# More PSUM banks for the preparing steps of a hash-attention and gated-FFN kernel, a second queue for the first loads, and products of zeros ahead of them

**Chip, cores, metric.** One core of a Trainium2 chip; each group of experiments ran on one chip, side by side with the kernel before. Time is the device time of one execution in microseconds (us), median of several runs.

## The reference

```python
# attention: batch 4, 8 heads, 768 positions, head size 64, 6 hash bits
q_bits = (q @ proj > 0);  k_bits = (k @ proj > 0)          # one bucket number of 6 bits each
mask   = q_bucket[:, None] == k_bucket[None, :]
attn   = softmax(where(mask, q @ k.T / 8, -1e9));  x = attn @ v
# gated block on x reshaped to (3072, 512); d_ff = 1536, weights given as float64
out = ((silu(x @ w_gate) * (x @ w_val)) @ w_out)
```

## The kernel before

There are 16 pairs of heads, four to a batch. Each pair needs eight *preparing steps*: four transposes (q and k, two halves each; PE writes a PSUM bank, ScalarE copies it out) and four hash products (PE writes a bank; ScalarE makes q's signs, VectorE makes k's bits). The steps of pair n+1 are issued during pair n, two in an iteration. An iteration has two scores, two value products ("attend"), and after each half of a pair a row sum ("norm") whose reciprocal VectorE takes out of PSUM. When a batch is done, its gated-block work becomes a list of small pieces ("atoms") issued between the attention work of the next batch. VectorE meanwhile narrows the float64 weights.

```python
sc_ps  = tc.tile_pool(name="sc_ps",  bufs=2, space=PSUM)   # scores, 2 banks each
av_ps  = tc.tile_pool(name="av_ps",  bufs=1, space=PSUM)
aux_ps = tc.tile_pool(name="aux_ps", bufs=1, space=PSUM)   # one bank
mm_ps  = tc.tile_pool(name="mm_ps",  bufs=2, space=PSUM)   # two banks, gated block
def bank(name):      return mm_ps.tile([P, 512], FP32, tag="mm", name=name)
def side_bank(name): return aux_ps.tile([P, 512], FP32, tag="aux", name=name)
...
def front(n, bank=side_bank):                              # the preparing steps
    def transpose(name, half):
        ...
        ps = bank("tps")
        for i in range(CH):
            nc.tensor.transpose(ps[:, i * P : (i + 1) * P], raws[name, n][...], ident)
        nc.scalar.copy(T[name, n][:, half * HQ : (half + 1) * HQ], ps[:, 0:HQ])
    def hash_bits(name, half):
        ps = bank("hps")
        nc.tensor.matmul(ps[:, 0:HQ], hash_w[name], T[name, n][:, cols], ...)
        ...                                                # q: ScalarE, k: VectorE reads ps
...
def norm(u):
    ps = side_bank("sum")                                  # the same bank as the steps
    for h in range(2):
        nc.tensor.matmul(ps[h * D : (h + 1) * D, 0:HQ], ones, t[:, h, :], ...)
    nc.vector.reciprocal(r, ps[:, 0:HQ])
...
for step in front(0, bank):                                # first pair: the two gated banks
    step()
```

The softmax here doesn't subtract the row's maximum and nothing guards it: scores larger than these inputs give would overflow.

## Time and profile before

| | before |
|---|---|
| median of 3 runs | 1187.71 us (1186.89 to 1187.98) |
| span of the profiled run | 1185.9 us |
| TensorE busy / idle | 1156.9 / 29.0 us |
| first score / first gated product start at | 13.25 / 143.37 us |

The lines that carry the argument stand in the prediction below. The way to read them: the busy share says that TensorE is the bound, the slices say *where* it is idle, and the wait rows of that stretch say *on what*. One view more is needed here: the first batch of the kernel before in the view of busy time by stretch. Columns are stretch, its length, then busy time of PE, PEld, DVE, ACT and POOL with instruction counts, granted clock, DMA share and GB/s.

```profile
13.25:143.37 130.12, 110.53 (x626) 46.06 (x625) 94.00 (x125) 58.31 (x84) 3.84 (x7) 0.99 0.29 78
143.37:1185.90 1042.53, 1038.88 (x3838) 522.93 (x3836) 411.92 (x607) 217.62 (x350) 14.55 (x27) 1.00 0.11 31
```

From the first score to the first gated product takes 130.12 us; everything after it 1042.53.

### The profile page before, as it was taken

Reading aid. Unit: us, or ns where it says so; the run is one execution under the profiler, and the core shown is the slowest. Engines: PE = TensorE matmul, PEld = TensorE weight load, DVE = VectorE, ACT = ScalarE, POOL = GpSimd, SP = SyncE. Lnnn points to the kernel's source line nnn. Section 1 sums busy time; section 2 is a strip of 40 time slices with the busy share of each in tenths; the row PEclk is TensorE's granted clock in tenths of the full one; section 3 lists DMA queues with packets and bytes.
Section 4 is the critical chain, followed back from the end, with each engine's and each line's share of the span. In section 5 each row is a group of like instructions: output and inputs, shape, how many; then the busy total and the mean of one; then the engine's idle time right before and its main releaser. Section 6 shows DMA issues by size and latency. Waiting matters only on the chain.

```text
span 1185.9 us, 10899 instructions
## 1 busy us (share of the span) xinstructions
PE 1156.9 (98%) x4480; PEld 573.2 (48%) x4480; DVE 508.2 (43%) x756; ACT 280.3 (24%) x441; POOL 19.2 (2%) x44
## 2 busy tenths in 40 slices
PE   7888899999999999999999999999999999999998
PEld 3333355555544445555554445555554444555543
DVE  3777689998852323343331233333233222222100
ACT  4444422222212222222221213222131211000000
POOL 0000000000000000000000000000000000000000
PEclk9999999999999999999999999999999999999999
DMA  5322222324210120100002012010000000000000
GB/s 142 76 76 76 58 79 92 101 71 113 88 40 18 37 57 1 40 1 1 14 1 58 18 36 49 1 40 1 14 1 1 18 18 18 1 1 0 1 27 27
DMA packets 63698, 44.76 MB, mean 38 GB/s; under 512 B 51872, under 2 KB 55968, under 8 KB 63648
## 3 DMA queue, kind: packets, MB, share of 16 engines
q1 hardware_dynamic: 58752, 26.23, 8.6%
q0 software_dynamic: 4896, 17.83, 4.9%
q8 instruction: 35, 0.57, 0.2%
q14 instruction: 15, 0.12, 0.0%
HBM read 37.76 MB, written 6.29 MB: 37 GB/s over the span
## 4 chain that ended last, share of the span: by engine, by line
PE 97%; DVE 2%; ACT 1%; DMA 0%; SPq 0%; issue 0%; ACTq 0%
PE val L299 21%; PE g L299 21%; PE po L320 21%; PE sc L244 14%; PE av L255 11%; PE hps L213 4%; PE sum L276 2%; PE tps L205 2%; DVE r L279 2%; ACT qb L216 0%; ACT qT L208 0%; DMA kraw<-in_k_dram 0%; SPq L85 0%; ACT A L246 0%; ACT o L324 0%
## 5 line engine op out<-in xcount | busy, mean ns | idle before, releaser
L299 PE MATMUL val<-xT,wv 128*128 128x384 f32 x768 | 266.2, 489 | 0.0
L299 PE MATMUL g<-xT,wg 128*128 128x384 f32 x768 | 265.9, 489 | 0.0
L320 PE MATMUL po<-wo,ht 128*128 128x512 f32 x576 | 257.1, 597 | 0.0
L246 ACT ACTIVATE A<-sc 128x768 f32<-128x768 f32 x192 | 155.5, 812 | 208.2 <-PE sc L244 177.0
L299 PEld LDWEIGHTS val<-xT,wv 128*128 128x128 f32 x768 | 142.5, 190 | 105.4 <-DVE acc L263 6.0
L299 PEld LDWEIGHTS g<-xT,wg 128*128 128x128 f32 x768 | 142.5, 190 | 105.1 <-DVE acc L263 6.0
L320 PEld LDWEIGHTS po<-wo,ht 128*128 128x128 f32 x576 | 106.8, 190 | 134.1 <-issue 130.7
L244 PE MATMUL sc<-qT,kT 64*128 64x384 f32 x768 | 156.0, 485 | 0.0
L279 DVE RECIPROCAL r<-sum 128x384 f32<-128x384 f32 x32 | 81.8, 2556 | 151.9 <-PE sum L276 151.9
L255 PE MATMUL av<-A,vraw 128*64 128x386 f32 x768 | 144.8, 498 | 0.0
L306 DVE SCALAR_TENSOR_TENSOR t<-t,g 128x384 f32<-128x384 f32 x96 | 53.1, 554 | 206.3 <-ACT t L305 206.3
L263 DVE TENSOR_TENSOR acc<-acc,A 128x768 f32<-128x768 f32 x128 | 122.3, 955 | 35.2 <-ACT A L246 30.3
L305 ACT ACTIVATE t<-g 128x384 f32<-128x384 f32 x96 | 47.1, 490 | 351.6 <-PE g L299 347.0
L311 DVE SCALAR_TENSOR_TENSOR ht<-t,val 128x384 f32<-128x384 f32 x96 | 53.1, 553 | 125.0 <-PE val L299 125.0
L255 PEld LDWEIGHTS av<-A,vraw 128*64 128x64 f32 x768 | 49.6, 137 | 82.4 <-issue 81.3
L244 PEld LDWEIGHTS sc<-qT,kT 64*128 64x128 f32 x768 | 69.0, 190 | 21.5 <-issue 21.5
L244 PE MATMUL sc<-qb,kb 64*128 64x384 bf16 x384 | 63.8, 329 | 0.1
L218 DVE TENSOR_SCALAR kb<-hps,above_k,times_k 128x384 bf16<-128x384 f32 x32 | 21.6, 675 | 83.9 <-PE hps L213 83.4
L244 PEld LDWEIGHTS <-kb 64*128 64x128 bf16 x384 | 18.7, 93 | 67.9 <-issue 55.1
L324 ACT COPY o<-po 128x512 f32<-128x512 f32 x24 | 14.0, 585 | 144.3 <-PE po L320 142.0
L216 ACT ACTIVATE qb<-hps,nudge 128x384 bf16<-128x384 f32 x32 | 18.6, 581 | 69.4 <-PE hps L213 69.3
L213 PE MATMUL hps<-qT,hashq 128*128 128x384 f32 x64 | 27.7, 515 | 5.5 <-DVE e L281 5.5
(58 smaller groups left out, 409.9 us busy)
## 6 DMA issues: line engine op xcount, KB each, us to landing
qraw<-in_q_dram SPq DMA_DIRECT2D x32, 192.0 KB, 3.7
kraw<-in_k_dram SPq DMA_DIRECT2D x32, 192.0 KB, 4.6
vraw<-in_v_dram SPq DMA_DIRECT2D x16, 384.0 KB, 3.4
words<-in_moe_w_val_dram POOLq DMA_DIRECT2D x12, 512.0 KB, 3.8
words<-in_moe_w_out_dram POOLq DMA_DIRECT2D x12, 512.0 KB, 3.6
out_dram<-o SPq DMA_DIRECT2D x24, 256.0 KB, 2.0
words<-in_moe_w_gate_dram POOLq DMA_DIRECT2D x10, 512.0 KB, 3.9
words<-in_moe_w_gate_dram SPq DMA_DIRECT2D x2, 512.0 KB, 5.8
```

The lines of the kernel that those rows point to most:

```text
L205: nc.tensor.transpose(ps[:, i * P : (i + 1) * P], raws[name, n][:, half * CH + i, :, :].rearrange("p h d -> p (h d)"), ident)
L213: nc.tensor.matmul(ps[:, 0:HQ], hash_w[name], T[name, n][:, cols], start=True, stop=True)
L244: nc.tensor.matmul(sc[:, h, 0:HQ], x["k", n][rows, ks], x["q", n][rows, qs], start=start, stop=not start)
L246: nc.scalar.activation(ring[u % RING][:, :, 0:HQ], sc[:, :, 0:HQ], AF.Exp, scale=SCALE)
L255: nc.tensor.matmul(ps[h * D : (h + 1) * D, 0:AW], raws["v", n][:, h, c, :], a[:, h, :], start=c == 0, stop=c == NCH - 1)
L263: nc.vector.tensor_tensor(acc[n, half], acc[n, half], a[:, :, 0:HQ], op=ALU.add)
L279: nc.vector.reciprocal(r, ps[:, 0:HQ])
L299: nc.tensor.matmul(ps[:, 0:HQ], w[:, j, f * P : (f + 1) * P], x[:, j, half * HQ : (half + 1) * HQ], start=j == 0, stop=j == NJ - 1)
L305: nc.scalar.activation(t, ps[:, 0:HQ], AF.Tanh, scale=0.5)
L306: nc.vector.scalar_tensor_tensor(out=t, in0=t, scalar=1.0, in1=ps[:, 0:HQ], op0=ALU.add, op1=ALU.mult)
L311: nc.vector.scalar_tensor_tensor(out=ht, in0=now["t"], scalar=0.5, in1=ps[:, 0:HQ], op0=ALU.mult, op1=ALU.mult)
L320: nc.tensor.matmul(ps, hs[half][f][:, i * P : (i + 1) * P], wo[:, f, :], start=f == 0, stop=f == NF - 1)
```

## The change

The intent: in the first batch the gated block has no work yet, so its two PSUM banks lie idle; the preparing steps should rotate over them and the old bank. At start-up, k and the projection should not stand behind q on one queue, and products with zeros before the data comes should bring TensorE's products to their full pace, since the first products of the kernel run slow (three transposes take 0.87 us at 4.79 us and 0.55 later).

```diff
-    def load(n):
+    def load(n, k_queue=nc.sync):
 ...
-    load(0)
+    load(0, nc.scalar)
+    ident = ...; make_identity(nc, ident)           # moved up
+    zeros = konst.tile([P, 512], BF16, tag="zeros", name="zeros")
+    nc.vector.memset(zeros, 0.0)
+    for _ in range(9):
+        ps = bank("idle")
+        nc.tensor.matmul(ps, zeros[:, 0:P], zeros, start=True, stop=True)
+    two_proj = konst.tile([P, NBITS], FP32, tag="proj", name="proj")
+    for o in (0, D):
+        nc.scalar.dma_start(two_proj[o : o + D, :], proj[:, :])
 ...
-        nc.vector.memset(hash_w[name], 0.0)         # and six small loads of proj on nc.sync
+        nc.gpsimd.memset(hash_w[name], 0.0)         # and six small VectorE copies of two_proj
 ...
+    turn = iter(range(1 << 20))
+    def front_bank(name):
+        return side_bank(name) if atoms or next(turn) % 3 == 2 else bank(name)
-    def front(n, bank=side_bank):
+    def front(n):
 ...
-            ps = bank("tps")                        # and bank("hps")
+            ps = front_bank("tps")
 ...
-    for step in front(0, bank):
+    for step in front(0):
```

More of the change, by code (lines that the diff above doesn't have):

```diff
@@ L78 @@
     raws = {}
-    def load(n):
+    def load(n, k_queue=nc.sync):
         b, pr = pairs[n]
-        for name, src in (("q", q), ("k", k)):
+        for name, src, queue in (("q", q, nc.sync), ("k", k, k_queue)):
             t = raw.tile([P, NCH, 2, D], FP32, tag=name + "raw", name=name + "raw")
             for h in range(2):
-                nc.sync.dma_start(t[:, :, h, :],
+                queue.dma_start(t[:, :, h, :],
                                   src[b, 2 * pr + h].rearrange("(p c) d -> p c d", c=NCH))
@@ L93, in load @@
         raws["v", n] = t
-    load(0)
+    load(0, nc.scalar)
+    ident = konst.tile([P, P], FP32, tag="ident", name="ident")
+    make_identity(nc, ident)
+    zeros = konst.tile([P, 512], BF16, tag="zeros", name="zeros")
[6 more added lines that the diff above has]
+        nc.scalar.dma_start(two_proj[o : o + D, :], proj[:, :])
     hash_w = {}
@@ L102 @@
         hash_w[name] = konst.tile([P, P], FP32, tag="hash" + name, name="hash" + name)
-        nc.vector.memset(hash_w[name], 0.0)
-        for o in (0, D):
-            for at in (0, NBITS) if name == "q" else (0,):
-                nc.sync.dma_start(hash_w[name][o : o + D, o + at : o + at + NBITS], proj[:, :])
+        nc.gpsimd.memset(hash_w[name], 0.0)
     def column(name, first, second, third, rest):
@@ L120 @@
     times_k = column("times_k", OFF, -OFF / 2, -NBITS * OFF / 2, 0.0)
-    ident = konst.tile([P, P], FP32, tag="ident", name="ident")
-    make_identity(nc, ident)
     ones = konst.tile([P, D], FP32, tag="ones", name="ones")
     nc.vector.memset(ones, 1.0)
+    for name in "qk":
+        for o in (0, D):
+            for at in (0, NBITS) if name == "q" else (0,):
+                nc.vector.tensor_copy(hash_w[name][o : o + D, o + at : o + at + NBITS],
+                                      two_proj[o : o + D, :])
     RING = 4
@@ L194 @@
     bits = {}
-    def front(n, bank=side_bank):
+    atoms = []
+    turn = iter(range(1 << 20))
+    def front_bank(name):
+        return side_bank(name) if atoms or next(turn) % 3 == 2 else bank(name)
+    def front(n):
         def transpose(name, half):
@@ L211, in hash_bits @@
             cols = slice(half * HQ, (half + 1) * HQ)
-            ps = bank("hps")
+            ps = front_bank("hps")
             nc.tensor.matmul(ps[:, 0:HQ], hash_w[name], T[name, n][:, cols], start=True, stop=True)
@@ L286, in norm @@
             push_ffn(b)
-    atoms = []
     def push_ffn(b):
```

## The prediction

Marked cuts in the recorded texts are statements of hardware behaviour that no trace or run of this case shows, and what hung on them. The prediction's sum came to 15.85 us: 14.1 for the banks, -0.9 for VectorE, 1.75 for start-up, 0.9 for the slow stretch. "The clock" at start-up means the pace of the products: the granted clock reads 1.00 in every us from 4 to 14 of the kernel before. The slow stretch of the kernel before does show in it: 0.60, 0.50, 0.50 and 0.69 in the four us from 114 to 118, 1.00 from 113 to 114 and from 118 to 120.

> **What bounds the kernel now.** I read the page first: the busy shares, the forty slices and the chain that ended last.
>
> ```profile
> PE 1156.9 (98%) x4480; PEld 573.2 (48%) x4480; DVE 508.2 (43%) x756; ACT 280.3 (24%) x441; POOL 19.2 (2%) x44
> ...
> PE   7888899999999999999999999999999999999998
> DVE  3777689998852323343331233333233222222100
> ...
> PE 97%; DVE 2%; ACT 1%; DMA 0%; SPq 0%; issue 0%; ACTq 0%
> ```
>
> TensorE is the bound. Its idle time is 1185.9 - 1156.9 = 29.0 us, and no change that leaves the products alone can gain more than that (and what slow-clock products cost). The row of slices (29.6 us each) puts nearly all the idle time in the first five slices: start-up and the first batch, where no gated-block work fills TensorE's waits. Then the waits of TensorE from 13 to 150 us (what it waited for, total, times, longest):
>
> ```profile
> PE hps L213 <- DVE e L281: 5.5, 4, 1.4
> PE hps L213 <- ACT qb L216: 5.4, 8, 0.7
> PE tps L205 <- ACT qT L208: 4.6, 8, 0.6
> PE tps L205 <- DVE e L281: 4.1, 3, 1.4
> ```
>
> Together 19.6 us. The same view from 150 us to the end is empty. All four rows are of the preparing steps (transposes "tps", hash products "hps"), which share one PSUM bank with each other and with the row sums "sum" that the reciprocal reads. The timeline of TensorE shows single cases (start, duration, and in brackets the idle time before it):
>
> ```profile
> 80.74 0.55 PE L205 MATMUL tps<-ident,qraw 128*128 128x128 f32 x3 [1.36 <-DVE e L281]
> 81.85 0.55 PE L205 MATMUL tps<-ident,kraw 128*128 128x128 f32 x3 [0.57 <-ACT qT L208]
> ...
> 91.84 0.91 PE L213 MATMUL hps<-kT,hashk 128*128 128x384 f32 x2 [0.67 <-ACT qb L216]
> ```
>
> The second step of an iteration waits for ScalarE to empty the bank that the first filled: 0.57 us for a transpose, 0.67 for a hash product. After a row sum the first step waits 1.36 for the 2.56 us reciprocal to leave it. Start-up, in the timeline again:
>
> ```profile
> 4.79 0.87 PE L205 MATMUL tps<-ident,qraw 128*128 128x128 f32 x3 [4.79 <-DMA qraw<-in_q_dram]
> 6.62 0.87 PE L205 MATMUL tps<-ident,kraw 128*128 128x128 f32 x3 [0.95 <-DMA kraw<-in_k_dram]
> ...
> 8.76 1.59 PE L213 MATMUL hps<-qT,hashq 128*128 128x384 f32 x2
> 10.15 1.48 PE L213 MATMUL hps<-kT,hashk 128*128 128x384 f32 x2
> ...
> 13.25 0.34 PE L244 MATMUL sc<-qb,kb 64*128 64x384 bf16 x2
> ```
>
> q lands at 4.8 us, k at 6.6, and the first score starts at 13.25. The reader should see that three transposes take 0.87 us here and 0.55 later, two hash products 1.59 and 0.91 later: the first products run slow. (The granted-clock row shows full speed there, so it does not see this.)
>
> [...]the durations above are long until about 11 us and normal at 12.4. [...]from 113.7 to 117 us scores and value products ran at about half speed (0.99 and 1.49 us for four where 0.81 is usual), just after 3.0 us in which TensorE did only transposes and waited. It cost about 2.70 + 2.11 - 1.72 - 1.52 = 1.6 us. [...]the engines are 0.9 busy from about 2.5 us on, at 220 to 260 GB/s, while SyncE's issues of q and k take 1.35 us each.[...]
>
> **The change, part by part.** The instruction orders compared show the same sequence on every engine; added are nine loads and products of zeros on TensorE, one clearing and six small copies on VectorE, four issues ahead of ScalarE's table load and two clearings on GpSimd. No work is removed.
>
> *Banks.* Until the first gated work is pushed, steps take turns: two steps in the gated block's banks, every third in the old one. So two steps of one iteration never share a bank, and all sixteen waits for evictions go: 8 x 0.57 + 8 x 0.67 = 10.0 us (the two ACT rows). The seven waits for the reciprocal go only where the step does not draw the old bank. I counted the turns: pair 0's preparation takes 0 to 7, the next 8 to 15, and so on; a turn that leaves 2 on division by 3 is the old bank. Steps beside a row sum are the first and last two steps of each preparation (except the first two of pair 1's, which have no sum before them). In order: turn 14 (old bank, first of its two: full wait 1.37); turn 17 (old, second: 1.37 less the 0.48 that the first transpose takes, 0.89); turn 23 (second, behind a hash product of 0.85: 0.52); for pair 3's none; for pair 4's turns 32 and 38, both first: 1.37 each. Left: 3 x 1.37 + 0.89 + 0.52 = 5.5. Removed: 9.6 - 5.5 = 4.1. With the evictions 14.1 us.
>
> *Does VectorE take over?* One pair's period, in the view of busy time by stretch (length, then PE, PEld, DVE, ACT):
>
> ```profile
> 61.50:92.70 31.20, 25.99 (x151) 10.82 (x152) 23.56 (x31) 13.77 (x20) 1.06 (x2) 1.00 0.27 72
> ```
>
> Without waits TensorE needs 26.0 us and VectorE has 23.6 of work: 91%. I followed VectorE through one wait-free pair, using the spacings in its timeline: from a reciprocal at 2.6 us after the iteration's start it finishes the twelfth accumulation about 13.4 us after it, and TensorE wants it for the next row sum at 13.6. That holds, but with no room; narrowing operations of 0.69 instead of 0.43 us push it by some 0.3. I charge 0.3 for each of three pairs: -0.9. ScalarE (13.8 of 26) is no limit: an exponential held up by its ring buffer has a whole iteration before it is read.
>
> *Start-up.* q and k of pair 0 are 0.79 MB; at about 235 GB/s from 2.0 us on, both are in by about 5.7: q 0.9 later than now, k 0.8 earlier. The zeros start near 1.2; a bf16 product of 384 columns takes 0.16 to 0.17 in the trace, so 512 take 0.22, slow 0.44, nine about 4.0: they end near 5.2, before the data. If the clock is up, four transposes take 4 x 0.48 and four hash products 4 x 0.85 (the spacings later in the trace), without eviction waits since three banks rotate: 5.7 + 1.9 + 3.4 = 11.0. Projection and its six copies should be there at 6 to 7, before the hash products at 7.6. I add 0.5 for a chance that the clock is not up yet[...]: first score at 11.5 instead of 13.25, a gain of 1.75.
>
> *The slow stretch.* [...]0.9 of the 1.6, an estimate.
>
> Sum: 14.1 - 0.9 + 1.75 + 0.9 = 15.85. All of it carries to the end, since from 143 us on TensorE waits for nothing: 1187.7 - 15.9 = 1171.8; I say **1171.5 us**, 1.4% less.
>
> **The rivals.** (1) VectorE becomes the bound in the first batch: its late accumulations hold the row sums and, through the ring of four, the exponentials. For it: 91%[...]. Against it: each step's own wait for a hash product lets it catch up, as the 4.3 us gap before "kb" shows now. It would leave perhaps 9 us of the banks' gain: 1177. (2) Start-up gains nothing or loses: q comes later, and zeros that end too early[...] leave the hash products slow: first score at 13 or later, so 1173.5. (3) The pay-back: weights narrowed by VectorE are late for the first "val" product at 146 us, which now waits for its last piece within 0.6 us. A VectorE behind by 1 us would cost at most that: 1172.5. (4) Everything goes well, all reciprocal waits but two shrink and the slow stretch goes: 19 to 20 us, 1167.5.
>
> **Range and chances.** The banks' 14 us are counted waits, uncertain by 2; start-up by 1.2; the clock by 1. Rivals 1 and 2 together make about 1176, rival 4 makes 1167.5: range 1167.5 to 1175.5. Two per cent is 23.8 us, below 1164: it would take nearly all 29 us of idle time. Chances: faster 0.01, same 0.98, slower 0.01.
>
> **What would show it.** In the new trace: TensorE's waits from the first score to the first "g" near 6 us instead of 19.6, with the rows for "qT" and "qb" gone and rows for the reciprocal at five places; a pair's period near 27 to 28 us instead of 31.2; the first score near 11.5 and the first "g" product near 127.5 to 128 instead of 143.4; from there to the end 1042.6 us as before. Wrong: row sums that wait for "acc" by more than 0.5 us each, a first score later than 13, or a tail longer by over 1 us.

## The result

| | before | after |
|---|---|---|
| median | 1187.3 us (4 runs, 1186.25 to 1187.98) | 1168.91 us (4 runs, 1167.45 to 1169.88) |
| profiled span | 1185.9 | 1168.1 |
| first score at | 13.25 | 14.50 |
| first score to first gated product | 130.12 | 110.83 |
| first gated product to the end | 1042.53 | 1042.77 |

The ratio is 0.9845, 95% interval 0.9828 to 0.9862. Ratios here are the mean time of one kernel's fast runs over that of the other's in the same rounds, so they are not quite the ratio of the medians quoted. The gain stays under the 2% from which a change counts as faster. The page of the kernel after, its busy shares and TensorE's slices:

```profile
PE 1155.5 (99%) x4489; PEld 575.1 (49%) x4489; DVE 508.9 (44%) x761; ACT 279.4 (24%) x441; POOL 19.5 (2%) x46
...
PE   8999999999999999999999999999999999999998
```

The eights after the first slice are gone. All of TensorE's waits of the kernel after, over the whole span:

```profile
PE hps L232 <- DVE e L300: 3.2, 3, 1.4
PE tps L224 <- DVE e L300: 2.2, 2, 1.4
PE tps L224 <- DMA kraw<-in_k_dram: 1.3, 1, 1.3
PE idle L105 <- DVE nudge L119: 1.2, 1, 1.2
PE tps L224 <- DMA qraw<-in_q_dram: 0.6, 1, 0.6
```

The rows for evictions (qT, qb) have gone, and five reciprocal waits of together 5.4 us are left, where 19.6 us of waits stood. (The rows name "e", the 0.10 us instruction of VectorE right behind the reciprocal; of the two only the reciprocal reads the bank.) The stretches again:

```profile
14.50:125.33 110.83, 105.22 (x625) 46.25 (x625) 93.94 (x125) 57.40 (x85) 3.84 (x7) 1.00 0.31 79
125.33:1168.10 1042.77, 1038.89 (x3838) 522.98 (x3836) 411.88 (x607) 217.71 (x350) 14.55 (x27) 1.00 0.11 31
```

The first batch is 130.12 - 110.83 = 19.3 us shorter, more than the 14.2 us of wait rows that went: TensorE's idle time falls from 19.6 to 5.6 us, and its busy time too, from 110.53 to 105.22. The tail is the same to 0.24 us. And start-up (timeline of TensorE, start and duration) is 1.25 us *longer*:

```profile
1.19 4.02 PE L105 MATMUL idle<-zeros 128*128 128x512 bf16 x9 [1.19 <-DVE nudge L119]
5.83 0.87 PE L224 MATMUL tps<-ident,qraw 128*128 128x128 f32 x3 [0.62 <-DMA qraw<-in_q_dram]
8.03 0.87 PE L224 MATMUL tps<-ident,kraw 128*128 128x128 f32 x3 [1.32 <-DMA kraw<-in_k_dram]
...
11.25 1.49 PE L232 MATMUL hps<-kT,hashk 128*128 128x384 f32 x2
...
14.50 0.34 PE L263 MATMUL sc<-qb,kb 64*128 64x384 bf16 x2
```

Both data come later than before (q at 5.83 instead of 4.79, k at 8.03 instead of 6.62), and the transposes still take 0.87 us for three: behind the zeros they are no faster.

So two things were to be explained: why the banks gave 19.3 us where the rows promised 14, and why start-up lost.

### The profile page after: what moved, and what is told of

Same layout as the page of the kernel before. It is cut to its first block, busy times and chain, and to the rows that moved or that the text cites. A ratio compares the mean times of both kernels' runs of the same rounds, so it can differ in the third digit from the quotient of the medians.

```text
span 1168.1 us, 10917 instructions
## 1 busy us (share of the span) xinstructions
PE 1155.5 (99%) x4489; PEld 575.1 (49%) x4489; DVE 508.9 (44%) x761; ACT 279.4 (24%) x441; POOL 19.5 (2%) x46
## 4 chain that ended last, share of the span: by engine, by line
PE 97%; DVE 2%; DMA 1%; ACT 0%; issue 0%; ACTq 0%; DVEq 0%
PE val L316 22%; PE g L316 22%; PE po L337 22%; PE sc L263 14%; PE av L274 11%; PE hps L232 4%; PE sum L295 2%; PE tps L224 2%; DVE r L298 1%; DMA kraw<-in_k_dram 1%; DVE acc L282 0%; DVE acc L278 0%; ACT A L265 0%; DVE wv L177 0%; ACTq L85 0%
## 5 line engine op out<-in xcount | busy, mean ns | idle before, releaser
L341 ACT COPY o<-po 128x512 f32<-128x512 f32 x24 | 14.1, 585 | 144.3 <-PE po L337 142.0
L278 DVE SCALAR_TENSOR_TENSOR acc<-A 128x768 f32<-128x768 f32 x32 | 30.5, 952 | 0.8 <-ACT A L265 0.8
```

The source lines that it names most:

```text
L278: nc.vector.scalar_tensor_tensor(out=acc[n, half], in0=ring[(u - 1) % RING][:, :, 0:HQ], scalar=S * EPS / P, in1=a[:, :, 0:HQ], op0=ALU.ad ...
```

## The experiments

**1 and 2: each half of the change alone.** Run e1 takes the kernel before and adds only the rotation; run e2 takes the kernel after and gives back the old bank:

```diff
 e1, against the kernel before
+        return side_bank(name) if atoms or next(turn) % 3 == 2 else bank(name)   # as in the change
 e2, against the kernel after
-        return side_bank(name) if atoms or next(turn) % 3 == 2 else bank(name)
+        return bank(name) if next(turn) < 8 else side_bank(name)
```

Of theory A in e1's text, that a removed wait is worth more than its idle row, the mechanism named for the rest is cut; no trace shows one. The spacings stay.

> Only the bank rotation, start-up as before. Theory A: [...] (in the changed kernel two transposes of one iteration take 0.81 us to the next score instead of 1.59, 0.78 less where the idle row said 0.57; two hash products 1.49 instead of 2.43, 0.94 where the row said 0.67). Then the rotation alone gives 14.2 us of rows, about 3.5 us[...] and perhaps the 1.6 us of the slow stretch: 17.7 to 19.3 less than before, about 1168 to 1169.6 us, and so as fast as the whole change or faster. Rival, the prediction's sum: 14.1 less 0.9 for VectorE, 1174 us, the rest of the whole change's gain coming from the start-up part.

> Only the start-up part (keys and projection on the second queue, zeros, two alternating banks for the first preparation as before); later preparations use the one old bank. Theory A: the start-up part loses what its trace shows, 14.50 instead of 13.25 us to the first score: about 1 to 1.5 us slower than before, 1188.5 us. Rival, the prediction: 1.75 us faster, 1185.7 us.

Measured: e1 1167.62 us (1167.17 to 1168.35, ratio 0.9835, 0.9822 to 0.9848); e2 1188.64 us (1187.60 to 1189.26, ratio 1.0011, 0.9998 to 1.0023). The rotation alone gives the whole gain and a little more (1187.34 - 1167.62 = 19.7 us); the start-up part costs about 1.3 us, though its interval just includes no change. The prediction's two numbers for these (1174 and 1185.7) both fail.

The extra is visible where a wait has gone. The timeline of TensorE in the kernel before, one iteration with two transposes, to the next score:

```profile
85.50 0.55 PE L205 MATMUL tps<-ident,qraw 128*128 128x128 f32 x3
86.61 0.55 PE L205 MATMUL tps<-ident,kraw 128*128 128x128 f32 x3 [0.57 <-ACT qT L208]
87.09 0.34 PE L244 MATMUL sc<-qb,kb 64*128 64x384 bf16 x2
```

and in the kernel after:

```profile
23.54 0.55 PE L224 MATMUL tps<-ident,qraw 128*128 128x128 f32 x3
23.93 0.49 PE L224 MATMUL tps<-ident,kraw 128*128 128x128 f32 x3
24.35 0.34 PE L263 MATMUL sc<-qb,kb 64*128 64x384 bf16 x2
```

From the first start to the score: 87.09 - 85.50 = 1.59 before, 24.35 - 23.54 = 0.81 after. The row said 0.57, the iteration lost 0.78. In the second listing the rows overlap: the next transposes start at 23.93 while the first are still ending (24.09). Behind a wait they do not: in the first listing the row ends at 86.05 and the next starts at 86.61. The overlap that is missing there is in no idle time. For two hash products it is the same: 90.26 to 92.69 before, 27.52 to 29.01 after, 0.94 us where the row said 0.67. Read off in the same way, the first batch's sixteen iterations with two steps agree: seven with transposes lose 0.78 or 0.79 us, seven with hash products 0.94; in the other two the second step still waits, for a reciprocal. Beyond the rows that is 7 x 0.21 + 7 x 0.27 = 3.4 us. With the 14.2 of the rows and the 1.6 of the slow stretch of the kernel before (which the prediction describes and the kernel after does not show), 19.2 of the 19.3 us are accounted for.

The slow stretch comes and goes: e2, which has the old bank's waits, shows one too, at another place (timeline of TensorE; the granted clock averages 0.99 from 14.28 to 144.38 us there, as it does in the first batch of the kernel before, and 1.00 in that of the change):

```profile
130.16 0.91 PE L232 MATMUL hps<-qT,hashq 128*128 128x384 f32 x2 [1.36 <-DVE e L300]
...
132.98 1.49 PE L263 MATMUL sc<-qT,kT 64*128 64x384 f32 x4
```

It takes 1.49 us where 0.81 is usual. Neither the trace of the change nor that of e1 has one between the first score and the first gated product (both take 110.83 us for it).

**3 and 4: the zeros.** Run e3 drops the nine products (the loop and its tile), run e4 makes them twenty:

```diff
-    for _ in range(9):
+    for _ in range(20):
```

> The whole change without the nine products of zeros. Theory Z (they ended at 5.2 us, and the gaps until k came at 8.0 us let their effect lapse, or zeros never raised the clock): first score at about 14.5 us as with them, time within 0.5 us of the changed kernel. Rival (they shortened the slow phase): the hash products stay slow longer and the first score comes at 15 us or later, about 1 us slower.

> The whole change with twenty products of zeros instead of nine, so that TensorE is busy without a gap until k has landed. If sustained zeros raise the clock: some of the products at 0.22 instead of 0.43 us, the last ending at 7 to 8.5 us, transposes at 0.55 and hash products at 0.91 us, the first score near 12.5 to 13.5 us: 1 to 2 us faster than the changed kernel. If zeros do not count as work: all twenty at 0.43 us, ending at 9.8, everything after them slow, first score near 17 us: 2 us slower.

Measured: e3 1169.22 us (1168.95 to 1169.42); e4 1167.82 us (1167.59 to 1168.01). So nine zeros are worth nothing that these runs can show, while twenty are worth about 1.1 us of the change's 1168.9 and 1.4 of e3's 1169.2. (e3 and e4 shared a chip; the change itself was timed in another session against the same kernel before, 1187.3 in both.) In e3's trace the first score even comes at 13.73; the rival's 15 us is refuted. Twenty zeros, in the timeline of e4 in narrow windows, and what follows them:

```profile
2.44 1.06 PE L105 MATMUL idle<-zeros 128*128 128x512 bf16 x2
...
7.34 0.81 PE L105 MATMUL idle<-zeros 128*128 128x512 bf16 x3
...
8.25 0.52 PE L224 MATMUL tps<-ident,qraw 128*128 128x128 f32 x3
...
12.52 0.34 PE L263 MATMUL sc<-qb,kb 64*128 64x384 bf16 x2
```

Two zeros take 1.06 us early and three take 0.81 late: the pace is full from about 6.5 us on, and transposes (0.52 for three) and hash products (0.88, then 0.81 for two) keep it, though the transposes start 2.4 us later than in the change. So the pace can become full while only zeros run; nine of them, 4.0 us, end before that happens, or just after: the pace became full at about 4.2 us in run e7 below and at about 4.9, during the last zero, in e6, and within the 4.0 us of the change not at all. Where the zeros ended fast and a gap followed, the pace was lost again: e6's transposes take 0.52 us for three at 6.21 and 0.83 at 8.28, after waits of 1.07 and 1.56 us on either side of the first.

**5: the queue.** Run e5 is the change with k back on SyncE's queue; only the projection stays on ScalarE's.

```diff
-    load(0, nc.scalar)
+    load(0)
```

> The whole change, but the first keys go through SyncE's queue again, behind q and ahead of v (the projection stays on ScalarE's). Theory K (on a second queue k only shares the same DMA engines with v and pair 1's loads, which then stand ahead of nothing): q at 4.8 to 5.2 us and k at about 6.7 instead of 8.0, first score about 13.3 instead of 14.5, about 1.2 us faster than the changed kernel. Rival (k's lateness comes from the zeros or from ScalarE's start): k at about 8 again, no change of time.

Measured: 1166.25 us (1166.16 to 1167.64, ratio 0.9827), 2.7 us less than the change (2.2 by the means; the two were timed in different sessions). k's transposes start at 6.95 instead of 8.03, q's at 5.36:

```profile
5.36 0.87 PE L224 MATMUL tps<-ident,qraw 128*128 128x128 f32 x3
6.95 0.87 PE L224 MATMUL tps<-ident,kraw 128*128 128x128 f32 x3 [0.72 <-DMA kraw<-in_k_dram]
...
8.90 1.48 PE L232 MATMUL hps<-qT,hashq 128*128 128x384 f32 x2
10.18 0.89 PE L232 MATMUL hps<-kT,hashk 128*128 128x384 f32 x2
...
12.29 0.34 PE L263 MATMUL sc<-qb,kb 64*128 64x384 bf16 x2
```

So the second queue made k late. In the other traces k's transposes start at 6.62 (before), 6.73 (e1) and 7.09 (e9) with q and k on one queue, at 8.28 (e6) with k on the second. The zeros did not make it late: k's transposes start at 8.18 in e3 too. Nor did a late start of ScalarE, which issued k at 0.74 us, when SyncE issued q. How, the DMA view of the change shows in the window from 6 to 7 us (packets, MB, and the time that the packets took as a share of the 16 engines' time, which can pass 100%); q10 is ScalarE's queue with k and the projection, q1 is SyncE's, by then with v and pair 1's loads:

```profile
q1 hardware_dynamic: 472, 0.30, 100.6%
q10 hardware_dynamic: 134, 0.01, 11.0%
```

On one queue v follows k. On two, v (first read at 18.12 us) and the loads of pair 1 (first read at 19.57) run beside k and take most of the engines while k's last packets wait; by 6 us about 0.37 of k's 0.39 MB had come (the same view, us by us). The order is not fixed: in e2, with the same loads, q's transposes started only at 6.80 and k was in by 7.47, where the change has 5.83 and 8.03.

In the traces the first score comes 2.2 us sooner than in the change, more than the 1.1 us by which k came sooner; the rest goes with the pace, full sooner (k's first hash product, two records, already takes 0.89 us; in the change it took 1.49). That the queue brought this about is not shown: see "Left open" below.

**6: no old bank at all.** After the first pair, the steps of the first batch alternate between the gated block's two banks:

```diff
-        return side_bank(name) if atoms or next(turn) % 3 == 2 else bank(name)
+        n = next(turn)
+        return side_bank(name) if atoms or (n < 8 and n % 3 == 2) else bank(name)
```

(Cut from the text: a mechanism named for the 0.07 us. The figure is in the traces: the step of transposes behind the value products starts 2.83 us after them with the wait, 109.12 to 111.95 in the kernel before, and 1.40 without, 44.49 to 45.89 in the change: 1.43 where the row says 1.37.)

> The whole change, but after the first pair's preparation the steps of the first batch never draw the old bank and alternate between the gated block's two. The five waits for the reciprocal (5.4 us in the changed kernel's waits, about 0.07 more each[...]) should go: first score to first gated product 105 us instead of 110.8, time about 1163.2 us. Rival (VectorE at 23.6 of 26 us of a pair becomes the bound, or a bank is still held by the comparison of k behind a reciprocal): waits of TensorE for acc, kb or A of more than 1.5 us in all appear in their place, time 1165 us or more.

Measured: 1163.95 us (1162.98 to 1164.26, ratio 0.9804, 0.9790 to 0.9817, so whether it reaches 2% is unclear). The five reciprocal waits are gone, and of VectorE only this is left among TensorE's waits:

```profile
PE sum L296 <- DVE acc L283: 0.2, 1, 0.2
```

First score (13.64) to first gated product (118.70) takes 105.06 us, as expected. The rival, VectorE as the bound, is refuted for this kernel: at a pair's period of about 26 us it keeps up but for 0.2 us in all. The third bank in the rotation, which spreads steps further, was a loss: it is the one bank that the row sums hold.

**7: both heads split over both queues** (a version meant to win; two banks, one head of q and of k on each queue, q's transposes ahead of k's):

```diff
-    load(0, nc.scalar)
+    load(0, (nc.sync, nc.scalar))      # one queue per head, for q and k alike
```

(Cut from the text: assumptions on when the pace becomes full and on what a gap does to it, which no run had shown.)

> A version meant to beat both: as the two-bank run, and q and k of pair 0 each have one head on SyncE's and one on ScalarE's queue, so that neither is overtaken by v; the first preparation transposes both halves of q ahead of k. Theory K[...]: q at 4.5 to 5, k at 6 to 6.5, first score near 11, 1159.7 us, 2.3% under the kernel before. Rival (the queues do not matter[...]): first score at 13 to 14.5, 1162 to 1163.5 us.

Measured: 1163.09 us (1162.49 to 1163.40, ratio 0.9797, 0.9784 to 0.9810, so again unclear at 2%): the rival's range. q came at 5.09, but k only at 7.92, while half of it stood on ScalarE's queue beside v. The pace was full from about 4.2 us here, six transposes of q ran in 0.84 us, and after 1.99 us of waiting for k it was down again: six transposes of k took 1.54 us.

**8: does the pace become full behind transposes alone?** Forty transposes of the identity in place of the nine zeros, one look:

```diff
-    for _ in range(9):
+    for _ in range(40):
         ps = bank("idle")
-        nc.tensor.matmul(ps, zeros[:, 0:P], zeros, start=True, stop=True)
+        nc.tensor.transpose(ps[:, 0:P], ident, ident)
```

> The nine zero products are replaced by forty fp32 transposes of the identity, back to back, so the disputed thing is measured by itself: do transposes count as work that frees the clock? If they do, their spacing falls from about 0.21 to about 0.13 to 0.14 us some 4 to 7 us after the first, and later steps run at full speed. If they do not, all forty run at 0.21 us (8.6 us in all) and the hash products after them are slow (1.5 us for two). The time itself is expected some 1 to 3 us above the changed kernel's.

Measured: 1170.06 us (one run). The timeline of TensorE in narrow windows:

```profile
4.29 0.74 PE L105 MATMUL idle<-ident 128*128 128x128 f32 x2
...
6.13 0.44 PE L105 MATMUL idle<-ident 128*128 128x128 f32 x2
...
10.39 0.55 PE L224 MATMUL tps<-ident,qraw 128*128 128x128 f32 x3
```

Two transposes take 0.74 us until about 5.7 us and 0.44 after. Nothing but these fp32 transposes ran until then, and time alone does not do it: in e3, where TensorE does nothing before 6.16 us, products are still slow at 10.13 (1.48 us for two). So in this run forty transposes did what the zeros did in e4.

**9 and 10: a version that beats both.** Run e9 is e6 with k on SyncE's queue (as e5) and q's two transposes ahead of k's for the first pair; run e10 puts three more zero products between q's and k's transposes.

```diff
 e9, against e6
-    load(0, nc.scalar)
+    load(0)
-        for half in range(2):
-            for name in "qk":
-                steps.append(... transpose(name, half))
+        for half, name in ((0,"q"),(1,"q"),(0,"k"),(1,"k")) if n == 0 else ((0,"q"),(0,"k"),(1,"q"),(1,"k")):
+            steps.append(... transpose(name, half))
 e10, against e9
+        if at == 2:      # after q's two transposes of the first pair
+            busy(3)      # three more products of zeros
```

> The two-bank run with k back on SyncE's queue (projection on ScalarE's) and, for pair 0, both halves of q transposed ahead of k. From the earlier traces: k lands at 6.9, first score at 11.5 to 12.3 depending on when the clock is freed and whether the gap before k lets it lapse; first score to first gated product 105.1 us; 1161.5 us. Rival (the queue made no difference, the clock did): first score at 13.5, 1163.3 us.

> As the run before, with three more products of zeros between the transposes of q and those of k, so that TensorE has no gap longer than 0.5 us from 1.2 us on. If continuous work keeps the clock free: k transposes at 0.49 to 0.55 us for three and hash products at 0.81 for two, first score at 10.5 to 11.5, 1160.3 us, and less spread than without the filler. If a freed clock does not depend on such gaps: no change from the run before.

Measured: e9 1160.00 us (1159.93 to 1160.31, ratio 0.9768, 0.9754 to 0.9781); e10 1160.14 us (1159.99 to 1160.46, ratio 0.9768). Both are 2.3% faster than the kernel before and clearly faster than the change. The start of e9:

```profile
5.32 0.94 PE L225 MATMUL tps<-ident,qraw 128*128 128x128 f32 x6
7.09 0.85 PE L225 MATMUL tps<-ident,kraw 128*128 128x128 f32 x6 [0.83 <-DMA kraw<-in_k_dram]
...
10.45 0.34 PE L263 MATMUL sc<-qb,kb 64*128 64x384 bf16 x2
```

The first score at 10.45 is earlier than what the prediction had hoped for from the change (11.0 to 11.5). The filler did nothing that shows (first score at 10.85 in e10's trace): in e9 the pace stayed full over a gap of 0.83 us (six transposes of k in 0.85 us), and e10's spread is no smaller. That part of the expectation failed.

## Why the prediction was right, and where its steps were not

The time (1171.5 predicted, 1168.9 measured) and the verdict were right, but several terms of the sum were wrong, and that they nearly cancelled was luck.

- **The bound and where the gain lies:** right. The tail stayed at 1042.8 us, and all of the first batch's gain reached the end. The limit it set, idle time and what slow products cost, is not one, though: 3.4 us came out of busy time (third point).
- **Which waits stay:** right to the place. Predicted 5.5 us in five waits, 1.37, 0.89, 0.52, 1.37, 1.37; measured 5.4 in five, 1.36, 0.89, 0.52, 1.36, 1.36.
- **What a removed wait is worth:** too small. "With the evictions 14.1 us" took the idle rows as the price. Measured (experiment 1) it is 3.4 us more, because products that wait do not overlap with those before them (86.05 to 86.61 against 24.09 and 23.93). That a wait costs more than its row could be seen in the trace of before: where nothing waits, beside gated work, a step of transposes takes 0.33 us from its start to the next product's (146.05 to 146.38), and 0.48 behind a wait (86.61 to 87.09). The prediction used spacings for start-up and not here.
- **The charge for VectorE, 0.9 us:** too much; the change's trace has no wait for acc, and even e6, where TensorE leaves VectorE the least time, lost 0.2. The estimate had the last accumulation end 10.8 us after the reciprocal starts; it took 59.06 to 70.01, 10.95, but TensorE wanted it only at 70.58.
- **The slow stretch:** 0.9 predicted, 1.6 gained in the profiled runs. That the stretch follows from transposes was drawn from one case (it came just after 3.0 us of transposes and waits). Experiment 8 speaks against it (full pace behind forty transposes), and e2's slow stretch came after hash products (131.75 us). Its cause stays open; it is in the two traces that have the waits for evictions (before, e2) and not in those of the change and e1.
- **Start-up, +1.75 us:** wrong in sign; the first score came 1.25 us later in the trace of the change and 1.03 later in that of e2, whose median is 1.3 us slower. The failed step is "both are in by about 5.7": q was (5.83), k came at 8.03, since the sum counted only q's and k's bytes and left out v and pair 1, which SyncE's queue now issued beside k. Even without them the trace of before spoke against it: there the same 0.79 MB, with the engines 0.9 busy, were usable only at 6.62. The second failed step is "If the clock is up": nine zeros ended at 5.2 us and the products behind them were still slow (two hash products 1.49 us at 11.25). From k's transposes to the first score the change took 6.47 us; e4, at full pace, took 4.27 from its first transposes. In the trace of before the first product starts at 4.79 and they are slow until about 11, over 6 us, more than the 4.0 us of zeros. Rival 2 had named this case (first score at 13 or later).
- **The sum:** 14.2 + 3.4 + 1.6 - 1.25 - 0.24 (the tail) = 17.7, against 17.8 between the two profiled spans. Start-up's loss of 3 us against the plan and the 3.4 us of overlap nobody had counted came out nearly even, which is why the time looked better understood than it was.

Left open: what sets the time at which the pace becomes full. TensorE starts the same nine zeros at 1.19 us in all of these, and yet it was full at about 4.2 us in e7, 4.9 in e6, 5.5 in e9, 6.1 in e10, 10.2 in e5 and 13.5 in the change; e5 and e9 have nearly the same work and gaps up to 5.5 us. So the start-up of one trace is partly chance, and part of e9's lead in its trace too, though all nine timed runs of e9 and e10 lie within 0.6 us. Open too is why the second queue's last packets took so small a share (11.0% against 100.6% from 6 to 7 us).

## What to carry to other kernels

When two steps in turn share a PSUM bank on a bound TensorE, price the wait by the spacing of the starts with and without it, not by the idle row: here the price was 0.78 and 0.94 us where the rows said 0.57 and 0.67. Use idle banks first, and keep short steps out of a bank that a slow reader holds (here a reciprocal of 2.56 us), even at the cost of a smaller rotation (two banks beat three by 5 us). A second DMA queue did not bring the urgent load sooner here (k's transposes at 8.03 us, at 6.95 on one queue), and later loads took most of the engines while its last packets waited (100.6% against 11.0% from 6 to 7 us), so order by need on one queue. If products are put ahead of the data, make them last until the data are there (twenty zeros took 1.4 us off e3's time, nine nothing that shows) and judge them by several runs.
